# Attention and two gated MLPs on one core: the second MLP's projections in seven block products of 288 tokens

## The chip, the cores and the metric

The kernel runs on one core of one Trainium2 chip. The core's engines have queues of their own: TensorE (PE; its weight loads are PEld), VectorE (DVE), ScalarE (ACT), GpSimd (POOL) and SyncE (SP), which here only issues DMAs. The metric is the device time of one execution in microseconds; the median of several runs counts.

## The reference

Three parts follow one another, all in float32 with float64 weights:

```
attn:  q, k, v (4 batches, 8 heads, 576 positions, 64); heads 0-3 see the last 32 positions,
       heads 4-7 every 4th of the last 128
x   =  attn as 2304 tokens x 512
MLP 1: xn = x / sqrt(mean(x*x) + 1e-6) * rms_g
       g = xn @ w_gate;  v = xn @ w_val          (512 -> 1536)
       x = (g * sigmoid(g) * v) @ w_out          (1536 -> 512)
MLP 2: g = x @ w_gate;  v = x @ w_val
       out = (sigmoid(g) * v) @ w_out
```

Both MLPs have weights of their own. All matmuls of the MLPs need float32's precision.

## The kernel before

**Products.** A float32 operand is kept as two parts, a rounded one ("hi") and the rest ("lo"), and a product is three matmuls: hi·hi, hi·lo, lo·hi, in the format fp32r. The weights come as float64 words; `weight` (L302) turns them into float32 on the chip: ACT squares (L332), VectorE has four operations (L338, L341, L344, L347), then ACT rounds (L354, "whi") and GpSimd subtracts (L358, "wlo"), on tiles of 128 × 512.

**Tiles.** Tokens go in six chunks of 384, numbered 0 to 5. Each MLP runs in two passes; a pass holds six tiles of 128 hidden values and takes all six chunks with them. So there are four passes of 36 steps. In a step (`mlp_step`, L792 by way of `proj`) PE makes g and then v with 12 matmuls of 384 columns each; ACT takes tanh of g (L811), VectorE multiplies (L814, L819, L823), ACT or VectorE rounds the result (L826, L828, "hh") and GpSimd subtracts (L830, "hl"). After it PE makes the y of the step before (L855). In the first MLP y has the weights as the stationary operand and 384 tokens as columns, twelve matmuls in four banks. In the second MLP the hidden tile is stationary and 512 outputs are the columns, nine matmuls in three banks, so that the result lies in rows and goes straight to DRAM. Sums of a first pass go to DRAM and come back in the second (`part_load` L873, `y_evac` L884 to L914).

**Attention.** The 48 groups (four batches, four pairs of heads, thirds of a batch's positions) run in the prelude and in the first pass, ahead of the chunk that needs them. One group is a chain: scores on PE (L555), masks on VectorE (L566), exp on ACT (L572), sums and reciprocal (L579, L580), the product with it on GpSimd (L585), transposes on PE (L600), a copy (L604), values on PE (L612), a copy (L631). After the last group of a chunk comes `x_norm`: squares on ACT (L656), three additions on GpSimd (L664), sums over partitions by six matmuls of one column (L672), the reciprocal root on VectorE and GpSimd (L688 to L710), its spreading (L713) and turning on PE (L729), then xn, xh, xl (L740, L746, L751).

**Order.** `Line.emit` is a list scheduler. Each operation has a planned cost and a due time; at every step the operation that can start first is emitted, and of those that start alike the one due first. The order of g, v and y on PE is fixed by a key ("PE order"); attention, `x_norm` and the weights are put between by their due times from the table PARAMS (lo1 to hi5 are the due times of the groups for chunks 1 to 5). Each engine works off its queue in the emitted order.

## Time and profile before

| | |
|---|---|
| median of 3 runs | 1074.43 us (1071.85 to 1074.86) |
| profiled execution | 1074.17 us |
| its span | 1072.4 us |
| mean granted clock of PE | 0.971 |
| busy: PE, DVE, POOL, ACT | 1031.4, 499.3, 403.2, 353.9 us |
| prelude, up to the first step | 0 to 65.41 us |
| first pass | 65.41 to 379.10 us |
| second pass | 379.10 to 612.52 us |
| third pass | 612.52 to 840.62 us |
| fourth pass and the end | 840.62 to 1072.40 us |

A pass without a stall has 36 steps; in the first pass attention is added. The span is what the profile's records cover; the execution's own time holds 1.8 us more. In a row of the timeline a matmul's duration overlaps that of its neighbours; its cost is the distance of starts. The granted clock (PEclk) is 1.00 at 2.4 GHz and 0.50 at 1.2 GHz. In names such as `g<-xh,whi` the output stands ahead of the arrow and the operands behind it.

### The profile page before, as it was taken

The numbers are of one execution on the slowest core, as the hardware profiler recorded it, in microseconds if no ns is written. First come the engines' busy times: TensorE is split into PE (matmuls) and PEld (weight loads), VectorE is DVE, ScalarE is ACT, GpSimd is POOL, SyncE is SP. The second block draws the span as 40 slices with busy tenths as digits, with TensorE's granted clock in tenths as the row PEclk, the third lists the DMA queues.
The fourth block names the chain that finished last, engine by engine and source line by source line (L and its number), as shares of the span: only waits on it lengthen the run. The fifth ranks groups of instructions, "written<-read, shape, count | busy, mean of one in ns | idle before, by whom it ended". The sixth has DMA issues, their size and how long they took to land.

```text
span 1072.4 us, 17094 instructions
## 1 busy us (share of the span) xinstructions
PE 1031.4 (96%) x6455; PEld 967.7 (90%) x6455; DVE 499.3 (47%) x1080; ACT 353.9 (33%) x930; POOL 403.2 (38%) x536
## 2 busy tenths in 40 slices
PE   7889699999999899999999899999999999999998
PEld 6668589898999899999999889999999999999997
DVE  4699875554388988882226894101101111110111
ACT  4757544545233333332124332112214211111111
POOL 4556855344443743332135751111116411111111
PEclk8759999999999999999999899999999999999999
DMA  7858557441245355574225353102201211321210
GB/s 162 194 154 168 123 159 150 92 106 40 96 152 188 113 187 190 183 273 149 79 89 181 126 195 138 64 26 89 89 25 64 89 59 60 118 94 43 99 59 30
DMA packets 143538, 125.90 MB, mean 117 GB/s; under 512 B 94304, under 2 KB 128096, under 8 KB 143456
## 3 DMA queue, kind: packets, MB, share of 16 engines
q1 hardware_dynamic: 143456, 124.81, 38.2%
q8 instruction: 51, 0.84, 0.3%
q14 instruction: 31, 0.25, 0.1%
HBM read 91.75 MB, written 33.03 MB: 116 GB/s over the span
## 4 chain that ended last, share of the span: by engine, by line
PE 83%; DVE 9%; DMA 2%; issue 2%; POOL 2%; SPq 1%; ACT 1%; DVEq 0%; POOLq 0%; ACTq 0%
PE g L792 26%; PE v L792 25%; PE y L855 25%; PE att L555 2%; DVE wz L341 2%; DVE wz L344 2%; PE att L612 2%; DVE wz L338 1%; PE att L600 1%; DVE wz L347 1%; SPq L388 1%; SPq L463 1%; PE y L612 0%; DVE big L897 0%; DVE t L814 0%
## 5 line engine op out<-in xcount | busy, mean ns | idle before, releaser
L830 POOL TENSOR_TENSOR hl<-t,hh 128x384 fp32r<-128x384 f32 x141 | 152.1, 1079 | 530.2 <-ACT hh L826 491.8
L792 PE MATMUL g<-xh,whi 128*128 128x384 f32 x576 | 198.3, 344 | 7.4 <-DVE t L814 7.4
L823 DVE SCALAR_TENSOR_TENSOR t<-t,v 128x384 f32<-128x384 f32 x72 | 39.8, 553 | 354.7 <-PE v L792 348.7
L792 PE MATMUL g<-xh,wlo 128*128 128x384 f32 x576 | 196.5, 341 | 3.6 <-POOL wlo L358 3.6
L792 PE MATMUL v<-xh,whi 128*128 128x384 f32 x576 | 195.7, 340 | 2.1 <-DVE t L823 1.7
L792 PE MATMUL g<-xl,whi 128*128 128x384 f32 x576 | 195.6, 340 | 0.0
L792 PE MATMUL v<-xh,wlo 128*128 128x384 f32 x576 | 193.2, 335 | 0.9 <-POOL wlo L358 0.9
L792 PE MATMUL v<-xl,whi 128*128 128x384 f32 x576 | 193.1, 335 | 0.0
L811 ACT ACTIVATE t<-g 128x384 f32<-128x384 f32 x144 | 70.6, 490 | 313.7 <-PE g L792 298.4
L826 ACT CAST hh<-t 128x384 fp32r<-128x384 f32 x119 | 61.1, 513 | 239.3 <-DVE t L823 147.1
L792 PEld LDWEIGHTS g<-xh,whi 128*128 128x128 f32 x576 | 110.1, 191 | 12.8 <-DVE t L814 8.0
L358 POOL TENSOR_TENSOR wlo<-wz,whi 128x512 fp32r<-128x512 f32 x72 | 103.9, 1458 | 28.1 <-ACT whi L354 21.0
L792 PEld LDWEIGHTS g<-xh,wlo 128*128 128x128 f32 x576 | 110.2, 191 | 3.9 <-POOL wlo L358 3.9
L792 PEld LDWEIGHTS g<-xl,whi 128*128 128x128 f32 x576 | 110.3, 191 | 3.1
L792 PEld LDWEIGHTS v<-xh,whi 128*128 128x128 f32 x576 | 108.9, 189 | 4.2 <-DVE t L823 2.5
L792 PEld LDWEIGHTS v<-xh,wlo 128*128 128x128 f32 x576 | 108.6, 188 | 1.2 <-POOL wlo L358 1.2
L792 PEld LDWEIGHTS v<-xl,whi 128*128 128x128 f32 x576 | 108.8, 189 | 0.0
L855 PE MATMUL y<-hh,whi 128*128 128x384 f32 x288 | 101.0, 351 | 1.2 <-DVE ys L884 1.2
L855 PE MATMUL y<-hh,wlo 128*128 128x384 f32 x288 | 96.4, 335 | 0.0
L855 PE MATMUL y<-hl,whi 128*128 128x384 f32 x288 | 96.4, 335 | 0.0
L855 PE MATMUL y<-whi,hl 128*128 128x512 f32 x216 | 85.6, 396 | 0.0
L855 PE MATMUL y<-wlo,hh 128*128 128x512 f32 x216 | 85.3, 395 | 0.0
(125 smaller groups left out, 1501.9 us busy)
## 6 DMA issues: line engine op xcount, KB each, us to landing
wst<-in_moe_w_gate_dram SPq DMA_DIRECT2D x24, 512.0 KB
wst<-in_moe_w_val_dram SPq DMA_DIRECT2D x24, 512.0 KB
wst<-in_moe_w_out_dram SPq DMA_DIRECT2D x24, 512.0 KB
xh<-xh SPq DMA_DIRECT2D x12, 768.0 KB
xl<-xl SPq DMA_DIRECT2D x12, 768.0 KB
xh<-yh SPq DMA_DIRECT2D x12, 768.0 KB
xl<-yl SPq DMA_DIRECT2D x12, 768.0 KB
yp<-ys SPq DMA_DIRECT2D x24, 192.0 KB
```

What stands on the lines that cost most here:

```text
L338: add("DVE", 0.34, lambda: nc.vector.tensor_scalar(out=z.t.bitcast(F32), in0=z.t.bitcast(F32), scalar1=LEAST * LEAST, scalar2=MANTISSA, op ...
L341: add("DVE", 0.6, lambda: nc.vector.scalar_tensor_tensor(out=z.t, in0=top(), scalar=3, in1=z.t, op0=ALU.logical_shift_left, op1=ALU.bitwis ...
L344: add("DVE", 0.6, lambda: nc.vector.scalar_tensor_tensor(out=z.t, in0=top(), scalar=-0x40000000, in1=z.t, op0=ALU.bitwise_and, op1=ALU.bit ...
L358: add("PL", 1.23, lambda: nc.gpsimd.tensor_tensor(out=lo.t, in0=z.t.bitcast(F32), in1=hi.t.bitcast(F32), op=ALU.subtract), reads=[zk, ("hi ...
L555: nc.tensor.matmul(out=sc.t[r, u, :], lhsT=qt.t[r, p0:p0 + QB], rhs=kt.t[r, p0:p0 + WIN], start=True, stop=True)
L612: nc.tensor.matmul(out=o.t[64 * e:64 * e + 64, QB * u:QB * u + QB], lhsT=vt.t[:, G * g + u, e0 + e, :], rhs=pts.t[:, u, 64 * e:64 * e + 64 ...
L792: nc.tensor.matmul(out=bank.t, lhsT=l.t[:, s], rhs=r.t[:, kk], start=kk == 0 and n == 0, stop=kk == KD - 1 and n == 2)
L811: add("ACT", 0.37, lambda: nc.scalar.activation(out=t.t, in_=gb.t, func=ACTF.Tanh, scale=0.5), reads=[("bank", p, c, f, 0)], writes=[key], ...
L823: add("DVE", 0.47, lambda: nc.vector.scalar_tensor_tensor(out=t.t, in0=t.t, scalar=1.0, in1=vb.t, op0=ALU.add, op1=ALU.mult), reads=[("ban ...
L826: add("ACT", 0.41, lambda: nc.scalar.copy(out=hh.t, in_=t.t), reads=[key], writes=[("hh", p, c, f)], tiles=[t, hh], due=s + 0.6, other=() ...
L830: add("PL", 0.98, lambda: nc.gpsimd.tensor_tensor(out=hl.t, in0=t.t, in1=hh.t.bitcast(F32), op=ALU.subtract), reads=[key, ("hh", p, c, f)] ...
L855: nc.tensor.matmul(out=yb.t, lhsT=l, rhs=r, start=first and j == 0, stop=last and j == 2)
```

## The change

The first MLP keeps its matmuls, its two passes and its chunks of 384 tokens (T1, NF1). The second MLP is new:

- **Three passes** (TWO) of four hidden tiles each (NF), over the four batches, whose 576 tokens are two halves of 288 (T). Every other pass takes the batches in the opposite order, so that a pass begins with the operands that the one before ended with.
- **Seven products for eight.** `unit` takes two hidden tiles and two halves. With two blocks of the 512 input values, each of g and v is a 2 × 2 by 2 × 2 block product. Strassen's scheme (in Winograd's form) makes it of seven block products with sums of weight blocks (S1 to S4, `weight_blocks`) and of token blocks (T1 to T4, `x_blocks`). A block product is six matmuls of 288 columns. The seven use the banks X, Z, X, Y, X, Y, X: X is the bank g or v, Z and Y are two banks of "att". Products that belong to the same result add up in the bank; `snap` copies a bank (ACT, or VectorE), `plus` adds one to a copy (VectorE), `finish` takes tanh or multiplies and splits.
- **y** (`y_group`) has the weights as the stationary operand in this MLP too, three matmuls of 288 columns. The y of one batch is put between the products of the next; the first two units have none. The result lies turned: VectorE transposes blocks of 32 × 32 (`out_blocks`), and four DMAs for each tile write runs of 32 numbers; the last half is turned by PE (`out_rows`).
- **Weights aside.** `weight_ahead` converts a weight and stores the float32 tile to DRAM, `weight_load` reads it back when it is needed. It is used for the second half of the first MLP's weights (18, converted in the first pass) and for all 36 of the second MLP (converted in the second pass). Splits into hi and lo happen behind the reading (`split`), on half tiles of 256.
- **The plan.** Due times are now in microseconds (STEP is 6.24 for a step), costs are closer to measured ones, and the DMA is modelled as one bus. The due times of the attention groups are the old ones in the new unit.

The core of the diff:

```diff
-    17.458, "lo5": 29.921, "hi5": 18.146, "lead": -2.417, "xdue": 1.161, "wdue": -1.154,
...
+    "hi4": 108.9, "lo5": 186.7, "hi5": 113.2, "lead": -15.1, "xdue": 7.2,
...
+    ONE, TWO = 2, 3
+    NF1 = DF // P // ONE
+    NF = DF // P // TWO
...
+    def weight_ahead(p, f, i, load_due, due, release=0.0):
+        z = words(p, f, i, load_due, due, release)
+        key = (layer_of(p), f, i)
+        z_scr[key] = dr.tile([P, CW], F32, name=f"z{layer_of(p)}_{f}_{i}")
+        dma(lambda: nc.sync.dma_start(out=z_scr[key], in_=z.t.bitcast(F32)), 262e3,
+            reads=[("z", key)], writes=[("zs", key)], tiles=[z], due=due + 3)
+    def weight_load(p, f, i, due, early=False):
+        key = (layer_of(p), f, i)
+        z = new("sb", "wst", [P, CW], F32, NST) if early else one_of(Z_HOMES, [P, CW], F32)
+        dma(lambda: nc.sync.dma_start(out=z.t, in_=z_scr[key]), 262e3,
+            reads=[("zs", key)], writes=[("z", key), "zl order"], tiles=[z], due=due,
+            release=EARLY * early)
+        return z
+    EARLY = 285.0
+    def weight_late(p, f, i, due, early=False):
+        z = weight_load(p, f, i, due - 6, early)
+        if i == 2:
+            weight_out(p, f, z, lambda: z.t, due)
+        else:
+            weight_halves(p, f, i, z, lambda: z.t, due)
+    ORDER = ("11", "12", "S2", "S1", "S3", "S4", "22")
...
+    def weight_blocks(p, f, i, due):
+
+        layer = layer_of(p)
+        z = [weight_load(p, f + e, i, due - 6) for e in range(2)]
+        zk = [("z", (layer, f + e, i)) for e in range(2)]
+        blk = lambda e, k: lambda: z[e].t[:, k * KW:(k + 1) * KW]
...
+        for name in ORDER:
+            if name == "S2":
+                combine("S1", blk(1, 0), blk(1, 1), ALU.add, [zk[1]], [z[1]])
+                combine("S2", of("S1"), blk(0, 0), ALU.subtract,
+                        [("S", p, f, i, "S1"), zk[0]], [s_of["S1"], z[0]])
+            elif name == "S3":
+                combine("S3", blk(0, 0), blk(1, 0), ALU.subtract, zk, z)
+            elif name == "S4":
+                combine("S4", blk(0, 1), of("S2"), ALU.subtract,
+                        [("S", p, f, i, "S2"), zk[0]], [s_of["S2"], z[0]])
...
+    RIGHT = ("11", "21", "T2", "T1", "T3", "22", "T4")
...
+        for name in RIGHT:
+            if name == "11":
+                combine(lambda: t3.t, blk(1, 1), blk(0, 1), [key(1, 1), key(0, 1)], [tk],
+                        [xq[1], t3])
+                combine(blk(0, 1), blk(0, 1), blk(0, 0), [key(0, 0)], [key(0, 1)], xq)
+            elif name == "T2":
+                combine(blk(0, 0), blk(1, 1), blk(0, 1), [key(1, 1), key(0, 1)], [key(0, 0)], xq)
+            elif name == "T4":
+                combine(blk(1, 0), blk(1, 0), blk(0, 0), [key(0, 0)], [key(1, 0)], [xq[0]])
...
+    def y_group(p, c, f, m, due):
...
+        def products():
+            s = slice(m * P, m * P + P)
+            for j, (l, r) in enumerate(((0, 0), (0, 1), (1, 0))):
+                nc.tensor.matmul(out=yb.t, lhsT=w.t[:, l, s], rhs=h.t[:, r],
+                                 start=n == 0 and j == 0, stop=n == nf - 1 and j == 2)
...
+    def out_blocks(c, m, due):
+        src = parts[LAST, c]
+        t = new("sb", "ys", [P, T])
+        blocks = lambda x: x.rearrange("p (n i) -> p n i", i=32)
+        add("DVE", 0.5, lambda: nc.vector.transpose(
+            out=blocks(t.t), in_=blocks(src.t[:, m])), reads=[("sum", LAST, c, m)],
+            writes=[("ob", c, m)], tiles=[src, t], due=due + 1)
+        rows = out[c * T:(c + 1) * T, m * P:(m + 1) * P].rearrange(
+            "(n i) (a f) -> a i n f", i=32, f=32)
+        for a in range(4):
+            dma(lambda a=a: nc.sync.dma_start(
+                out=rows[a], in_=blocks(t.t[32 * a:32 * a + 32])), 37e3,
+                reads=[("ob", c, m)], writes=[("out", c, m, a)], tiles=[t], due=due + 2)
...
+            def product(i, bank, key, first):
+                l, r = wt[p, f, which, ORDER[i]], xop[p, b, RIGHT[i]]
+                def run():
+                    for j in range(2):
+                        cols = slice(j * P, j * P + P)
+                        for m, (a, d) in enumerate(((0, 0), (0, 1), (1, 0))):
+                            nc.tensor.matmul(out=bank.t, lhsT=l.t[:, a, cols], rhs=r.t[:, d, j],
+                                             start=first and j == 0 and m == 0,
...
+            steps = (("X", lambda: snap("11", X, "X")),
+                     ("Z", lambda: (plus("11", Z, "Z"), finish("11"))),
+                     ("X", lambda: snap("12", X, "X")),
+                     ("Y", lambda: snap("22", Y, "Y")),
+                     ("X", lambda: (plus("22", X, "X"), finish("22"))),
+                     ("Y", lambda: (plus("12", Y, "Y"), finish("12"))),
+                     ("X", lambda: finish("21")))
+            banks = [key for key, _ in steps]
+            for i, (key, then) in enumerate(steps):
+                product(i, {"X": X, "Y": Y, "Z": Z}[key], key, key not in banks[:i])
+                at += 0.78
+                then()
+                n += 1
+                while done < total * n // 14:
+                    at += extra[done](at, which)
+                    done += 1
...
+        for n in range(3 * NF1):
+            f, i = divmod(n, 3)
+            t = (8 + 24 * n / (3 * NF1)) * STEP
+            weight_ahead(1, NF1 + f, i, t - 8, t, 57 + 1.2 * t)
+            weight_late(1, NF1 + f, i, (NC1 * NF1 + f + (1.66 if i == 2 else i * 0.33) - 2) * STEP,
+                        n < 6)
+        todo = [(p, NF * (p - ONE) + 2 * u + e, i) for p in range(ONE, ONE + TWO)
+                for u in range(NF // 2) for i in range(3) for e in range(2)]
+        for n, (p, f, i) in enumerate(todo):
+            t = (NC1 * NF1 + 4 + 29 * n / len(todo)) * STEP
...
+        extra, carry = [[] for _ in range(NF // 2)], []
+        for p in range(ONE, ONE + TWO):
+            f0 = NF * (p - ONE)
+            for n, b in enumerate(range(B) if (p - ONE) % 2 == 0 else reversed(range(B))):
+                if n or p == ONE:
+                    x_blocks(p, b, at - 26)
+                else:
+                    for name in RIGHT:
+                        xop[p, b, name] = xop[p - 1, b, name]
+                        xkey[p, b, name] = xkey[p - 1, b, name]
+                for u in range(NF // 2):
+                    if not n:
+                        for i in range(2):
+                            weight_blocks(p, f0 + 2 * u, i, at - 24 + 8 * i)
+                        for e in range(2):
+                            weight_late(p, f0 + 2 * u + e, 2, at - 6)
+                    at = unit(p, b, u, at, extra[u])
+                extra, carry = late(p, b, carry)
+        for n, fn in enumerate(sum(extra, []) + carry):
+            at += fn(at, n % 2)
+
```

The order changes at two places that matter. The first is PE in the first pass, between chunk 4 and chunk 5. Before, the last attention group's scores (L555) stand there, between the matmuls of y (L855):

```order
L855 MATMUL y_3084<-hh,wlo 128x384
L555 MATMUL att<-kT,qT 64x96 x6
L855 MATMUL y_3095<-hh,whi 128x384
L855 MATMUL y_3095<-hl,whi 128x384
L855 MATMUL y_3095<-hh,wlo 128x384
L612 MATMUL att<-pts,v 64x64 x6
L855 MATMUL y_3123<-hh,whi 128x384
```

The spread reciprocal roots of that chunk (`rb`) are turned much later, also between matmuls of y:

```order
L792 MATMUL v<-xh,wlo 128x384
L855 MATMUL y_3817<-hh,whi 128x384
L855 MATMUL y_3817<-hl,whi 128x384
L855 MATMUL y_3817<-hh,wlo 128x384
L729 MATMUL att<-ident,rb 128x128 x3
L855 MATMUL y_3824<-hh,whi 128x384
L855 MATMUL y_3824<-hl,whi 128x384
L855 MATMUL y_3824<-hh,wlo 128x384
```

After, PE's queue at the same place reads as follows; L700 are scores, L742 the transposes of the probabilities, L754 the values, L814 the sums over partitions, L870 the turn of the roots, L973 the first g and v of chunk 5, L1010 y:

```order
L1010 MATMUL y_4261<-h,wo 128x384 x3
L1010 MATMUL y_4269<-h,wo 128x384 x3
L1010 MATMUL y_4274<-h,wo 128x384 x3
L1010 MATMUL y_4279<-h,wo 128x384 x3
L700 MATMUL att<-kT,qT 64x96 x6
L742 MATMUL att<-ident,pr 96x128 x3
L754 MATMUL att<-pts,v 64x64 x6
L814 MATMUL att<-ones,pt 128x1 x3
L870 MATMUL att<-ident,rb 128x128 x3
L973 MATMUL g<-xo,w 128x384 x12
L973 MATMUL v<-xo,w 128x384 x12
L1010 MATMUL y_4261<-h,wo 128x384 x3
```

The five operations of attention and normalization stand in five rows that follow one another, and the first g of the chunk stands right behind them.

The second place is PE in the second MLP. Before, a step ends with v (the last three of its 12 rows are shown) and has the y of the step before, with the hidden tile `hh`, `hl` as one operand:

```order
L792 MATMUL v<-xh,whi 128x384
L792 MATMUL v<-xl,whi 128x384
L792 MATMUL v<-xh,wlo 128x384
L855 MATMUL y_8328<-whi,hh 128x512
L855 MATMUL y_8328<-wlo,hh 128x512
L855 MATMUL y_8328<-whi,hl 128x512
L855 MATMUL y_8334<-whi,hh 128x512
L855 MATMUL y_8334<-wlo,hh 128x512
```

After, the first unit starts right behind the first MLP's last y, and its products (L1147) follow one another, each in another bank than the one before:

```order
L1010 MATMUL y_6913<-h,wo 128x384 x3
L1010 MATMUL y_6922<-h,wo 128x384 x3
L1147 MATMUL g<-xo,w 128x288 x6
L1147 MATMUL att<-xo,w 128x288 x6
L1147 MATMUL g<-xo,w_5414 128x288 x6
L1147 MATMUL att<-xo,w_5419 128x288 x6
L1147 MATMUL g<-wst,w_5434 128x288 x6
L1147 MATMUL att<-wst,w_5480 128x288 x6
L1147 MATMUL g<-wst,w 128x288 x6
L1147 MATMUL v<-xo,w 128x288 x6
```

From the third unit on a group of y (L1010) stands behind each product:

```order
L1147 MATMUL g<-xo_7333,w 128x288 x6
L1010 MATMUL y_7573<-h,wo 128x288 x3
L1147 MATMUL att<-xo_7337,w 128x288 x6
L1010 MATMUL y_7590<-h,wo 128x288 x3
L1147 MATMUL g<-xo_7455,w_5414 128x288 x6
L1010 MATMUL y_7603<-h,wo 128x288 x3
```

Six matmuls of 288 columns take the place of twelve of 384, and three of 288 stand between them where nine of 512 stood behind two projections.

## Rows read from the trace of the kernel before

**Rows 1.** The page: the chain that ended last, by engine.

```profile
PE 83%; DVE 9%; DMA 2%; issue 2%; POOL 2%; SPq 1%; ACT 1%; DVEq 0%; POOLq 0%; ACTq 0%
```

**Rows 2.** Windows by chunk: us, busy (count) of PE, PEld, DVE, ACT, POOL; PEclk.

```profile
65.41:141.11 75.70, 65.16 (x516) 54.61 (x514) 71.72 (x186) 45.31 (x147) 59.98 (x85) 0.87 0.62 146
...
298.83:336.27 37.44, 37.44 (x218) 37.44 (x217) 32.87 (x50) 13.31 (x26) 13.38 (x12) 1.00 0.46 152
336.27:379.10 42.83, 39.48 (x218) 38.84 (x218) 38.59 (x46) 16.12 (x31) 27.93 (x19) 0.96 0.47 155
...
567.76:612.52 44.76, 40.44 (x217) 40.12 (x217) 35.31 (x42) 19.38 (x37) 31.50 (x24) 0.92 0.43 149
612.52:652.62 40.10, 38.23 (x203) 35.51 (x203) 36.05 (x46) 15.04 (x29) 18.79 (x15) 1.00 0.54 182
652.62:840.62 188.00, 188.00 (x992) 176.22 (x991) 22.80 (x39) 43.10 (x86) 47.88 (x45) 1.00 0.18 68
```

**Rows 3.** Timeline of PE in layer 2: start, us, line, operation.

```profile
799.55 0.33 PE L792 MATMUL v<-xl,whi 128*128 128x384 f32 x1
...
800.93 0.39 PE L855 MATMUL y<-whi,hh 128*128 128x512 f32 x1
...
802.09 0.40 PE L855 MATMUL y<-whi,hl 128*128 128x512 f32 x1
```

**Rows 4.** Timeline of PE at matmuls of one column.

```profile
217.69 0.72 PE L672 MATMUL att<-ones,big 128*128 128x1 f32 x6
218.28 0.42 PE L792 MATMUL g<-xh,whi 128*128 128x384 f32 x1
```

**Rows 5.** Windows of an idle stretch and of what follows it.

```profile
592.00:597.00 5.00, 0.88 (x6) 0.56 (x4) 4.93 (x5) 0.00 (x0) 2.68 (x2) 0.93 0.31 105
597.00:603.00 6.00, 5.80 (x18) 5.80 (x19) 5.72 (x8) 3.13 (x6) 4.50 (x3) 0.50 0.23 87
```

**Rows 6.** Timeline of one attention group and one normalization: start, us, engine, line.

```profile
234.82 0.71 PE L555 MATMUL att<-kT,qT 64*64 64x96 f32 x12
...
237.64 0.99 POOL L585 TENSOR_SCALAR pr<-pr,rs 128x96 f32<-128x96 f32 x3 [0.91 <-DVE rs L580]
...
237.68 0.49 PE L600 MATMUL att<-ident,pr 128*96 128x128 f32 x3
...
238.32 0.47 ACT L604 COPY pts<-att 96x384 f32<-96x384 f32 x1
...
278.41 0.94 ACT L656 ACTIVATE big<-xT 128x384 f32<-128x384 f32 x2
...
279.43 3.20 POOL L664 TENSOR_TENSOR big<-big 128x384 f32<-128x384 f32 x3 [1.13 <-ACT big L656]
...
283.77 0.72 PE L672 MATMUL att<-ones,big 128*128 128x1 f32 x6
...
289.15 0.55 DVE L713 COPY rb<-rsy 128x384 f32<-128x384 f32 x1 [3.37 <-POOL rsy L710]
...
296.93 0.49 PE L729 MATMUL att<-ident,rb 128*128 128x128 f32 x3
...
298.83 0.33 PE L792 MATMUL g<-xh,whi 128*128 128x384 f32 x1
```

**Rows 7.** Groups by form: busy us, mean ns, idle before.

```profile
L341 DVE SCALAR_TENSOR_TENSOR wz<-wst,wz 128x512 int32<-128x512 int32 x72 | 67.3, 935 | 1.8
...
L338 DVE TENSOR_SCALAR wz<-wz 128x512 f32<-128x512 f32 x72 | 51.1, 712 | 18.6 <-ACT wz L332 14.0 <-POOL wz L335 4.2
...
L604 ACT COPY pts<-att 96x384 f32<-96x384 f32 x38 | 17.9, 473 | 20.4 <-PE att L600 20.0
```

**Rows 8.** Timeline: the last matmul into a bank, and its reader.

```profile
804.95 0.33 PE L792 MATMUL g<-xh,wlo 128*128 128x384 f32 x1
...
805.38 0.49 ACT L811 ACTIVATE t<-g 128x384 f32<-128x384 f32 x1 [3.08 <-PE g L792]
```

**Rows 9.** Timeline of SP's queue: one issue of 128 short runs.

```profile
240.79 0.59 SPq L473 DMA_DIRECT2D v<-in_v_dram  x1
```

More of the change, by code (lines that the diff above doesn't have):

```diff
@@ L167, in emit @@
             o.end = start + cost + o.lat
+            if o.bus:
+                self.bus = max(self.bus, start + cost) + o.bus
+                o.end = self.bus + o.lat
             for t in o.tiles:
@@ new lines, in y_group @@
+    def y_group(p, c, f, m, due):
+        layer = layer_of(p)
+        nf, width, cost = (NF, T, 0.39) if layer else (NF1, T1, 0.52)
+        n = f % nf
+        if (p, c) not in ybank:
+            ybank[p, c] = [new("ps", f"y{i}", [P, width], F32, 1) for i in range(KD)]
+        yb, w, h = ybank[p, c][m], wo[layer, f], htile[p, c, f]
+        def products():
[3 more added lines that the diff above has]
+                                 start=n == 0 and j == 0, stop=n == nf - 1 and j == 2)
+        add("PE", cost, products, reads=[("wo", layer, f), ("hs", p, c, f)],
+            writes=[("y", p, c, m), "PE order"], tiles=[yb, w, h], due=due)
+        if n == nf - 1:
+            (y_evac if layer else y_first)(p, c, m, due + 0.4)
@@ new lines, in part_load @@
+    def part_load(p, c, due):
+        if p == 0:
+            return
+        if p == 1:
+            t = parts[p, c] = new("sb", "pt", [P, KD, T1], F32, 2)
+            dma(lambda: nc.sync.dma_start(out=t.t, in_=y_part[c]), 786e3,
+                reads=[("part", 0, c, m) for m in range(KD)],
+                writes=[("sum", p, c, m) for m in range(KD)] + ["pt order"], tiles=[t], due=due)
+            return
+        t = parts[p, c] = new("sb", "pt", [P, KD, T], F32, 2)
+        if p > ONE:
+            dma(lambda: nc.sync.dma_start(out=t.t, in_=o_part[c]), 590e3,
+                reads=[("part", p - 1, c)], writes=[("sum", p, c, m) for m in range(KD)] +
+                ["pt order"], tiles=[t], due=due)
@@ new lines, in out_rows, with turn @@
+    def out_rows(c, t, which, due):
+        p = LAST
+        src = parts[p, c]
+        bank = new("ps", "vg"[which], [TQ, KD, P], F32, 1)
+        row = one_of(Z_HOMES, [TQ, DM], F32)
+        def turn():
+            for m in range(KD):
+                nc.tensor.transpose(bank.t[:, m], src.t[:, m, t * TQ:(t + 1) * TQ], ident)
+        add("PE", 0.45, turn, reads=[("sum", p, c, m) for m in range(KD)] + ["ident"],
+            writes=[("ob", c, t), "PE order"], tiles=[src, bank], due=due)
+        add("ACT", act(DM), lambda: nc.scalar.copy(
+            out=row.t, in_=bank.t.rearrange("p m o -> p (m o)")), reads=[("ob", c, t)],
+            writes=[("row", c, t)], tiles=[bank, row], due=due + 0.5,
+            other=("ys", "DVE", dve2(DM), lambda: nc.vector.tensor_copy(
+                out=row.t, in_=bank.t.rearrange("p m o -> p (m o)"))))
+        r0 = c * T + t * TQ
+        dma(lambda: nc.sync.dma_start(out=out[r0:r0 + TQ, :], in_=row.t), 197e3,
+            reads=[("row", c, t)], writes=[("out", c, t)], tiles=[row], due=due + 1)
@@ new lines, in whole @@
+        steps = ONE * NC1 * NF1
+        for n in range(3 * NF1):
+            f, i = divmod(n, 3)
+            t = (8 + 24 * n / (3 * NF1)) * STEP
[4 more added lines that the diff above has]
+                for u in range(NF // 2) for i in range(3) for e in range(2)]
```

685 lines of the change are left out of this document (392 added, 293 removed), and 2 rows, old and new, of the table PARAMS.

## The prediction, made before the changed kernel had run

> **What bounds the kernel now.** I read the chain that ended last first: 83% of it is TensorE's own matmuls and 9% is VectorE [rows 1]. So the time is the matmuls' columns plus the places where PE is kept waiting. The windows by chunk say where those places are [rows 2]. The row 652.62:840.62 (the last five chunks of the third pass) has PE busy 188.00 of 188.00 us at full granted clock: nothing but columns counts there. The row 298.83:336.27 is a layer-1 chunk without a stall, 37.44 us. Against these two, 336.27:379.10 (the last chunk of the first pass) is 5.4 us too long, 567.76:612.52 (the last of the second) 7.3 us, and 612.52:652.62 (the first of the third) 40.10 − 188.00/5 = 2.5 us. In all three VectorE is busy for 35 to 39 us: it converts the next pass's weight words there. The first row, 65.41:141.11, is 75.70 us long with VectorE busy 71.72: the first chunk is bound by VectorE, not by PE.
>
> The timeline gives the price of a column [rows 3]: eight matmuls of 384 columns from 799.55 to 800.93, 0.1725 us each, and five of 512 from 800.93 to 802.09, 0.232 each, so 0.449 and 0.453 ns per column with no fixed part to be seen. A matmul of one column cannot hide its weight load, and six of these take 0.59 us, 0.098 each [rows 4].
>
> **The second MLP's matmuls.** Before, a step has 24 matmuls of 384 columns and nine of 512, and there are 72 steps: 995,328 columns. After, 24 units have 14 products of six matmuls (2016), and 1152 more make y, all of 288 columns: 912,384 columns. That is 11/12: seven products for eight on the two thirds that are projections. Thirty steps in 188.00 us [rows 2] are 6.267 a step, 451.2 for 72; 11/12 of it is 413.6, **−37.6 us**, at 0.1306 us a matmul. The trace has no matmul of 288 columns with a full weight load. Its bounds: the load alone, 0.098 [rows 4], lies under 0.1306 and so cannot lengthen it; at the worst a matmul stays at the 0.1725 of 384 columns, 546 us, or +95. I take 0.1306, since the rows at 384 and 512 fall on one line through zero.
>
> A rule of the Trainium skill speaks against that. "TensorE: Matmul & The Clock Gate", section "Back-to-back issue gap", gives about 81 ns a matmul at 128 columns and 131 at 512 in a stream with weight loads, so a large part that does not shrink with the columns. By a straight line between these (an estimate from that page) layer 2 would take about 284 us before and 323 after: the 22% more matmuls would cost 40 us. The rows disagree, with 232 ns at 512.
>
> **Weights aside.** Layer 2's 36 weights, and 18 of layer 1, are now converted earlier (18 during the first pass, 36 during the second), stored to DRAM and read back. Four VectorE operations of 0.71 to 0.94 us [rows 7], about 3.5 us a weight, are as many as before; what changes is where they stand. In the second pass they are now spread, six per 37.4 us chunk (21 us of VectorE), so the stalls at the two boundaries, 7.3 + 2.5, should go; I leave 3 us for the start of the new stage, in which PE waits for the first turned banks and combinations: **−7**. The last chunk of the first pass loses its 5.4 us of waiting for conversions but still takes on splits: **−4**. In the first chunk VectorE keeps nearly all of its work (one conversion fewer, 3.5 us, others in place): −1.5. In chunks 1 to 3 fewer conversions save some, and chunk 1's normalization costs 3: its sums and its turn of the roots now have 1.9 us of matmuls between them, where 5.9 are needed [rows 6] and 5.5 stood before: −1. Together **−2.5**, between −8 and +6.
>
> **The last attention group.** This is a loss which the order of PE shows. Before, the last scores, the last sums and the last turn of the reciprocal roots stand in three places with tens of matmuls between. After, the last group's scores, its turn, its values, the sums and the turn of the roots follow one another on PE, with chunk 5's first g right behind and nothing between. Every link is then bare [rows 6]: scores at 234.82 to the end of the probabilities at 238.63, 3.8 us; transposes at 237.68 to the copy's end at 238.79, 1.1; values and their copy, about as long, 1.0; two squares 0.94; three GpSimd additions 3.20; the sums at 283.77 to the end of the spread roots at 289.70, 5.9; the turn at 296.93 to the first g at 298.83, 1.9. With a tenth of a microsecond for each of six hand-overs that is 18.4 us, of which PE works about 2. So some 16.5 us stand idle, and then the clock: after the idle stretch 592 to 597 the granted clock was 0.50 (1.2 GHz) for the next 6.0 us [rows 5], which gives away 3.0 us; I take 2. **+18.5.** Bounds: 14, if the additions start beneath the squares and the clock costs nothing, and 22 with the whole 3.0 and slower additions; a gain is excluded, since before waits for nothing there. What VectorE and GpSimd do of the weights in that time is counted in the chunk terms.
>
> **Turning banks over.** In a product's sequence the g or v bank is used four times, and between two uses there is one other product (6 × 0.1306 = 0.78 us) plus, from the third unit on, y work of the same length: 1.57. To turn a bank over, its reader starts 0.43 us after the start of the last matmul [rows 8], 0.30 after its end, and a copy of 384 elements takes 0.473 [rows 7], so 0.77 and a semaphore. In the first two units that is no slack at all in 16 places; a cast or a tanh ahead of the copy adds its 0.49 [rows 8]. I take 0.2 each, 3 us. In the other 176 places 0.8 us are to spare, one operation ahead in the queue is hidden and two are not; I take 4 us. **+7**, between 0 and +45 (0.25 each on 176).
>
> VectorE's turned output stands off PE. Its 112 transfers of 128-byte runs do not: SP needs 0.59 us for an issue with 128 runs [rows 9], these have 288, and 52 issues stand in the last 31 us, about all that SP can do. Behind the last chunk only three row transfers remain. **+1**, between 0 and +3.
>
> **Sum**, against the profiled execution's 1074.17 us (span 1072.4, and 1.8 around it): −37.6 − 7 − 4 − 2.5 + 18.5 + 7 + 1 = −24.6, that is 1049.6. The median of the runs shown, 1074.43, is 0.3 above that execution. **I forecast 1050 us.**
>
> **The rivals.** *The gap is given back.* VectorE and GpSimd work off in it what PE would wait for in other chunks, the boundaries lose all their 9.8 us, chunk 5 its 5.4, the other chunks 8, and no bank waits: 1074.2 − 37.6 − 9.8 − 5.4 − 8 + 14 + 1 = 1028. For it: PE waits in the first pass mostly for VectorE's conversions, which don't wait for PE; against it: conversions stand far ahead of the gap by then, and the first chunk, the worst, lies before it. Half-way cases reach 1042. Chance 0.17.
>
> *The banks wait more.* Mean waits of 0.12 us at 192 places are 23 instead of 7, so 1066 us, and with 0.15 it is 1072. For it: copies, tanh and casts share ACT, in order, and a bank is used again sooner than a projection's was; against it: in layer 2 ACT was busy 43 of 188 us [rows 2]. Chance 0.16, of which 0.05 within 0.3% of before.
>
> *The banks decide (the slower side).* Same place, but each of the 192 turnovers finds a reader queued behind an operation of about half a microsecond, 0.30 us on the mean: 58 instead of 7, 1101 us. The point from which the kernel is slower is 0.16 us a turnover (7 + 24.5 us over 192). Against it: 0.8 us of spare in 176 of them. Chance 0.07.
>
> *The narrow matmul does not shrink in full.* At 0.1384 us (6% more) the saving falls to 12.8 and with the chain's loss the change ends even; at 0.145, 459 us, it is 1095. The rows speak against it. Chance 0.03.
>
> **How the numbers follow.** The forecast itself, 1042 to 1061, has 0.57. 0.3% of 1074.4, 3.2 us, is about what a measurement can tell from no change. Faster than that: 0.57 + 0.17 + 0.11 = 0.85; within it 0.05; slower 0.07 + 0.03 = 0.10. The range that holds 8 in 10 leaves out the lower half of the first rival and the slower cases: 1034 to 1073.
>
> **What would show it.** Right: in layer 2 matmuls of 288 columns 0.130 apart; PE idle for 15 to 18 us in one stretch ahead of chunk 5 of the first pass, with a granted clock of 0.5 behind it; the second pass's last chunk near 37.4 us; layer 2 from its first product to the end near 424 us; waits of PE for ACT or VectorE copies in it below 10 us in sum. Wrong: a spacing over 0.138; PE waiting at most turnovers; PE at work under the last group's chain; the first pass more than 20 us above 314 (141.11 − 65.41 and the chunks behind it to 379.10).

## The result, and the profile after

The changed kernel takes 1080.6 us (median of 5, 1078.2 to 1082.3), 1.0059 times the kernel before (95% interval 1.0037 to 1.0080): slower by 0.6%, where 1050 us had been forecast. The profiled execution took 1078.5 us, with a span of 1076.7 us, 4.3 more than before.

The page's chain by engine, to be held against [rows 1]:

```profile
PE 71%; DVE 12%; DMA 4%; SPq 4%; issue 4%; POOL 3%; ACT 2%; DVEq 0%; POOLq 0%; ACTq 0%
```

PE's share of the chain fell from 83% to 71%: its matmuls have fewer columns in all, and it waits more. The windows say where; the columns are those of [rows 2], the first four rows are chunks 3, 4 and 5 of the first pass and the last chunk of the second, the next the first two units, the rest of the second MLP, and the end:

```profile
257.51:297.98 40.47, 40.47 (x254) 39.55 (x253) 24.78 (x52) 13.49 (x32) 16.38 (x26) 1.00 0.40 137
297.98:357.92 59.94, 46.24 (x307) 43.11 (x307) 21.01 (x56) 15.76 (x46) 16.79 (x33) 0.88 0.30 101
357.92:399.07 41.15, 40.49 (x216) 39.56 (x217) 12.62 (x22) 14.11 (x33) 18.49 (x21) 0.92 0.42 135
...
587.85:628.63 40.78, 40.11 (x229) 39.47 (x229) 37.77 (x52) 18.53 (x42) 30.90 (x29) 1.00 0.51 156
...
628.63:660.00 31.37, 24.37 (x168) 22.49 (x168) 28.54 (x44) 14.55 (x34) 21.11 (x16) 1.00 0.29 98
660.00:1070.46 410.46, 403.58 (x3015) 398.52 (x3013) 243.49 (x454) 168.77 (x401) 195.91 (x193) 1.00 0.31 93
1070.46:1076.70 6.24, 0.27 (x3) 0.01 (x1) 0.00 (x0) 0.64 (x2) 0.00 (x0) 0.79 0.53 130
```

Chunk 4 is 22.5 us longer than the 37.44 of an undisturbed one. Of these 18.6 are a bare chain at its end; the other 3.9 are the matmuls of two more attention groups, which the kernel before had in earlier chunks. The first MLP ends at 628.6 us, where it ended at 612.5 before. The second MLP takes 448.1 us to the end of the span against 459.9: of the 37.6 us expected for its matmuls, 11.8 came. In its first two units PE is idle for 7 of 31.4 us, while VectorE is busy for 28.5.

The bare chain ahead of chunk 5, on PE (start, duration, line, operation, and the idle time before it with what ended it):

```profile
339.34 0.71 PE L700 MATMUL att<-kT,qT 64*64 64x96 f32 x12
342.57 0.96 PE L742 MATMUL att<-ident,pr 128*96 128x128 f32 x3 [2.52 <-POOL pr L730]
344.09 0.91 PE L754 MATMUL att<-pts,v 96*64 96x64 f32 x12 [0.56 <-ACT pts L746]
349.60 1.44 PE L814 MATMUL att<-ones,pt 128*128 128x1 f32 x6 [4.60 <-POOL pt L806]
355.72 0.87 PE L870 MATMUL att<-ident,rb 128*128 128x128 f32 x3 [4.67 <-DVE rb L855]
357.92 0.69 PE L973 MATMUL g<-xo,w 128*128 128x384 f32 x1 [1.33 <-ACT xo L402]
```

From 339.34 to 357.92 it is 18.6 us, link by link as [rows 6] had it (3.8 to the probabilities, 3.1 for the additions, 6.0 from the sums to the spread roots). Behind it the granted clock was at half speed, 0.50 for 6.3 us; most of that lies in chunk 5:

```profile
339.80:356.20 16.40, 4.03 (x31) 3.01 (x26) 2.02 (x12) 2.91 (x10) 6.31 (x18) 0.62 0.24 85
356.20:362.50 6.30, 4.31 (x12) 2.99 (x11) 4.05 (x6) 2.05 (x4) 2.00 (x2) 0.50 0.47 152
```

A bank that is turned over late, in unit 3 (timelines of VectorE, of GpSimd and of PE):

```profile
689.86 1.42 DVE L404 CAST h<-t 128x288 fp32r<-128x288 f32 x1
691.20 0.44 DVE L1159 COPY t<-v 128x288 f32<-128x288 f32 x1
...
689.46 1.65 POOL L406 TENSOR_TENSOR xo<-T,xo 128x576 fp32r<-128x576 f32 x1
...
691.70 0.53 PE L1147 MATMUL v<-xo,w 128*128 128x288 f32 x2 [0.44 <-DVE t L1159]
```

The last matmul into bank v had ended by 689.7. VectorE could copy the bank only at 691.20, since it had begun a cast that takes 0.31 us by itself and took 1.42 beside GpSimd's subtraction; PE waited. The same picture stands in units 5, 11, 13, 19 and 21. Over the second MLP all gaps on PE sum to 20.5 us, 9.2 of them in the first two units. Nearly all of it, 19.4 us, lies at 23 places. Seventeen of these, 14.9 us with the slow restarts described below, end with a copy on VectorE (L1159), which does only 29 of the 144 copies. ScalarE (L1157) does the other 115, and three waits, 1.6 us, end with one of them. The view of PE's waits, which leaves out short ones and counts from a matmul's modelled end, shows the same order (us in total, times, longest):

```profile
PE v L1147 <- DVE t L1159: 4.4, 7, 1.6
PE g L1147 <- DVE t L1159: 3.1, 1, 3.1
PE att L1147 <- DVE t L1159: 1.9, 1, 1.9
...
PE g L1147 <- ACT t L1157: 0.4, 1, 0.4
```

The spacing of the new matmuls, in the run of y at the end:

```profile
1056.06 12.16 PE L1010 MATMUL y<-h,wo 128*128 128x288 f32 x90 [0.42 <-DVE pt L1077]
1068.06 0.63 PE L1113 MATMUL v<-ident,pt 128*96 128x128 f32 x3
```

These are 90 matmuls in 12.00 us, of which 0.11 is the slow restart described below: 0.132 us each.

### The profile page after: what moved, and what is told of

Read it like the earlier page. It is cut to its first block, busy times and chain, and to the rows that moved or that the text cites. A ratio compares the mean times of both kernels' runs of the same rounds, so it can differ in the third digit from the quotient of the medians.

```text
span 1076.7 us, 20044 instructions
## 1 busy us (share of the span) xinstructions
PE 1006.9 (94%) x7254; PEld 964.7 (90%) x7254; DVE 695.7 (65%) x1479; ACT 458.0 (43%) x1231; POOL 503.7 (47%) x659
## 4 chain that ended last, share of the span: by engine, by line
PE 71%; DVE 12%; DMA 4%; SPq 4%; issue 4%; POOL 3%; ACT 2%; DVEq 0%; POOLq 0%; ACTq 0%
PE y L1010 23%; PE g L973 12%; PE v L973 11%; PE att L1147 9%; PE g L1147 6%; PE v L1147 5%; SPq L612 1%; PE att L700 1%; DVE t L1180 1%; SPq L659 1%; PE att L754 1%; DVE h L404 1%; DVE wz L389 1%; DMA wst<-in_moe_w_val_dram 1%; DVE h L409 1%
## 5 line engine op out<-in xcount | busy, mean ns | idle before, releaser
L1010 PE MATMUL y<-h,wo 128*128 128x288 f32 (+1 forms) x2016 | 369.9, 313 | 2.0 <-POOL h L406 1.0
L1010 PEld LDWEIGHTS y<-h,wo 128*128 128x128 f32 x2016 | 318.5, 188 | 4.6 <-POOL h L406 1.6
L406 POOL TENSOR_TENSOR h<-t,h 128x288 fp32r<-128x288 f32 (+1 forms) x149 | 146.1, 983 | 303.8 <-ACT h L402 238.9
L973 PE MATMUL g<-xo,w 128*128 128x384 f32 x864 | 170.8, 345 | 5.5 <-DVE t L987 2.5
L973 PE MATMUL v<-xo,w 128*128 128x384 f32 x864 | 163.8, 337 | 0.0
L973 PEld LDWEIGHTS g<-xo,w 128*128 128x128 f32 x864 | 154.2, 193 | 10.0 <-DVE t L987 3.2
L973 PEld LDWEIGHTS v<-xo,w 128*128 128x128 f32 x864 | 150.4, 188 | 1.5
L1147 PE MATMUL att<-xo,w 128*128 128x288 f32 x576 | 92.7, 296 | 0.8
L1164 DVE TENSOR_TENSOR t<-t,att 128x288 f32<-128x288 f32 x96 | 43.4, 452 | 65.3 <-PE att L1147 61.6
L1147 PEld LDWEIGHTS att<-xo,w 128*128 128x128 f32 x576 | 81.4, 188 | 2.2 <-DVE t L1159 2.2
L392 DVE SCALAR_TENSOR_TENSOR wz<-wst,wz 128x512 int32<-128x512 int32 x72 | 67.7, 940 | 1.4
L1147 PE MATMUL v<-xo,w 128*128 128x288 f32 x396 | 64.1, 297 | 2.9 <-DVE t L1159 2.8
L717 ACT ACTIVATE pr<-pr,nmx 128x96 f32<-128x96 f32 x144 | 52.6, 367 | 28.5 <-DVE nmx L711 28.3
L1147 PE MATMUL g<-xo,w 128*128 128x288 f32 x396 | 63.2, 295 | 0.0
L395 DVE SCALAR_TENSOR_TENSOR wz<-wst,wz 128x512 int32<-128x512 int32 x72 | 60.5, 840 | 1.5
```

The costliest lines, as they stand in the source:

```text
L392: add("DVE", dve(CW), lambda: nc.vector.scalar_tensor_tensor(out=z.t, in0=top(), scalar=-0x40000000, in1=z.t, op0=ALU.bitwise_and, op1=ALU ...
L395: add("DVE", dve(CW), lambda: nc.vector.scalar_tensor_tensor(out=z.t, in0=low(), scalar=29, in1=z.t, op0=ALU.logical_shift_right, op1=ALU. ...
L406: add("PL", pool(n), lambda: nc.gpsimd.tensor_tensor(out=lo(), in0=src(), in1=hi().bitcast(F32), op=ALU.subtract), reads=reads, writes=[ke ...
L717: add("ACT", PARAMS["exp_cost"], lambda u=u: nc.scalar.activation(out=pr.t[:, u], in_=pr.t[:, u], func=ACTF.Exp, bias=nmx.t[:, u:u + 1], s ...
L973: nc.tensor.matmul(out=bank.t, lhsT=w[:, l, cols], rhs=x[:, r, j], start=kk == 0 and n == 0, stop=kk == KD - 1 and n == 2)
L1010: nc.tensor.matmul(out=yb.t, lhsT=w.t[:, l, s], rhs=h.t[:, r], start=n == 0 and j == 0, stop=n == nf - 1 and j == 2)
```

## The experiments

Ratios are to the kernel before, measured beside it on the same chip; PE's gaps in the second MLP are summed over the trace (distances of starts over 0.2 us, less 0.132; in e12_tail 1.6 us for twelve transposes that stand between are left out).

| run | median us | ratio, 95% interval | gaps in MLP 2, us (first two units) |
|---|---|---|---|
| changed kernel | 1080.6 | 1.0059 [1.0037, 1.0080] | 20.5 (9.2) |
| e1_chain | 1069.8 | 0.9962 [0.9940, 0.9984] | 24.3 (12.4) |
| e2_no_dve_split | 1074.8 | 1.0017 [0.9996, 1.0037] | 16.0 (7.6) |
| e4_eight | 1095.1 | 1.0203 [1.0173, 1.0233] | 0.0 |
| e5_recost | 1076.6 | 1.0018 [0.9999, 1.0037] | 23.6 (8.4) |
| e6_no_sums | 1072.7 | 0.9987 [0.9973, 1.0000] | 15.5 (6.8) |
| e7_replan | 1079.8 | 1.0057 [1.0036, 1.0077] | 29.6 (7.8) |
| e8_release | 1061.7 | 0.9887 [0.9872, 0.9901] | 19.6 (8.0) |
| e9_copies_first | 1050.8 | 0.9789 [0.9772, 0.9806] | 7.7 (4.3) |
| e10_first_nodve | 1051.2 | 0.9789 [0.9775, 0.9804] | 7.2 (2.4) |
| e11_first_alone | 1071.7 | 0.9983 [0.9967, 0.9999] | 13.7 (10.3) |
| e12_tail | 1048.9 | 0.9774 [0.9758, 0.9791] | 7.8 (4.3) |

My theory after the result: three faults of order (the bare chain, conversions that run into the last steps, and copies queued behind slower work) took back what the products saved. The rival: the seven products need more of VectorE than there is, in whatever order.

**The price of a matmul and of a cast, by themselves (p1_widths).**

```diff
+WIDTHS = (512, 384, 288, 256, 320, 352, 448, 192, 288, 384, 512)
+ROUNDS = 16
...
+        for n in WIDTHS:
+            for r in range(ROUNDS):
+                bank = banks[r % 4]
+                for j in range(6):
+                    c = slice((j % 4) * P, (j % 4) * P + P)
+                    nc.tensor.matmul(out=bank[:, 0:n], lhsT=w[:, c], rhs=x[:, 0:n],
+                                     start=j == 0, stop=j == 5)
```

> A probe instead of the kernel: back-to-back matmuls with a 128x128 weight tile each and 192 to 512 columns, 96 of a width; beside them VectorE casts and additions of 128x288, first alone, then with GpSimd subtracting beside them. It computes nothing of the reference. Theory (a column has one price): 288 columns 0.130 us, 384 0.173, 512 0.231, and 192 0.087 or the weight load, about 0.1, whichever is longer. Rival (each matmul has a part that does not shrink): 288 columns 0.132 or more, 192 columns well over 0.09. For VectorE: a cast from SBUF to SBUF takes 0.31 us alone and about 1.2 with GpSimd beside it; one that reads a PSUM bank stays at 0.45. Rival: GpSimd makes no difference and the long casts of the changed kernel had another cause.

This probe ran once. The spacing is taken from the starts of the first and the last of 96 matmuls at a granted clock of 1.00 (for 512 columns from the second set, since the first twelve matmuls of the probe came 0.427 us apart):

```
columns   192     256     288     320     352     384     448     512
us        0.111   0.120   0.132   0.147   0.160   0.173   0.203   0.227
```

The rival holds: 288 columns cost 0.132, not 0.130. From 448 to 352 columns the price is 0.45 ns a column; at 288 it is 0.458, at 256 0.469, at 192 0.58: the fewer columns, the less is saved. VectorE in the same run (groups by line: count, busy us, mean ns):

```profile
L51 DVE CAST d<-raw 128x288 fp32r<-128x288 f32 x16 | 12.3, 768 | 0.5
L53 DVE TENSOR_TENSOR e<-raw 128x288 f32<-128x288 f32 x12 | 11.9, 1060 | 0.0
...
L46 DVE CAST d<-raw 128x288 fp32r<-128x288 f32 x24 | 5.4, 308 | 4.2 <-DMA raw<-in_q_dram 4.2
L56 DVE TENSOR_TENSOR e<-raw,zb 128x288 f32<-128x288 f32 x12 | 4.5, 444 | 0.0
```

L46 is the cast alone (308 ns), L51 the same cast beside GpSimd (768), L53 an addition of two SBUF operands beside GpSimd (1060), L56 one with a PSUM operand, also beside GpSimd (444). The theory holds in direction; the 1.2 us of the cast is 0.77 on the mean here.

**The bare chain (e1_chain).**

```diff
-    "hi4": 108.9, "lo5": 186.7, "hi5": 113.2, "lead": -15.1, "xdue": 7.2,
+    "hi4": 108.9, "lo5": 113.2, "hi5": 168.0, "lead": -15.1, "xdue": 7.2,
```

> The changed kernel with the due times of chunk 5's attention groups rising (113 to 168 us) instead of falling (187 to 113), so that the last group no longer stands alone on PE ahead of chunk 5. Theory (the bare chain costs its whole length): the 18 us between 340 and 358 in which PE works for 2 us go, and the half-clock behind them: about 1061 us, 19 less than the changed kernel. Rival (VectorE and GpSimd used the gap for work that PE would wait for otherwise): at most 6 us less, about 1075.

The windows of chunks 3, 4 and 5 and of the second pass's last chunk in this run:

```profile
260.61:304.57 43.96, 43.96 (x308) 42.01 (x307) 29.45 (x71) 17.97 (x49) 18.75 (x32) 1.00 0.38 127
304.57:345.37 40.80, 40.58 (x254) 39.55 (x253) 20.40 (x42) 12.07 (x29) 15.84 (x28) 1.00 0.52 181
345.37:383.69 38.32, 37.73 (x217) 37.41 (x217) 9.90 (x18) 12.54 (x30) 16.80 (x20) 1.00 0.33 110
571.78:619.80 48.02, 42.30 (x230) 41.09 (x229) 45.42 (x60) 20.36 (x45) 35.85 (x32) 0.94 0.58 187
```

Chunks 3 to 5 together fell from 141.6 to 123.1 us: the chain, with the half clock behind it, cost 18.5. (Chunk 4 alone fell by 19.1, but two groups of attention went back from it into chunk 3.) But the second pass's last chunk grew from 40.8 to 48.0, with VectorE busy for 45.4 of it. In sum the gain is 10 us by the ratios, between theory and rival. The conversions of the second MLP may not start before a fixed planned time, so they did not move with the rest.

**Conversions earlier too (e8_release).**

```diff
-            weight_ahead(p, f, i, t - 8, t, t + 135)
+            weight_ahead(p, f, i, t - 8, t, t + 108)
```

> As the run with chunk 5's due times rising (e1_chain, 1069.8 us), with the earliest start of the second MLP's conversions 27 us earlier (t + 108 instead of t + 135). Theory (taking away the bare chain gained 19 us in its chunk and lost 10 at the end of the second pass, since the conversions are held back to a fixed time and ran into the last steps there): the last chunk of the second pass goes from 48.0 to about 39 us, 1061 us in all. Rival (VectorE has that work to do there anyway): 47 to 48 us, 1068 to 1071.

The result is 1061.7 us, and the last chunk of the second pass took 42.4 us instead of 48.0; the theory holds, if not quite to 39.

**Hidden values never split by VectorE (e2_no_dve_split).** The split of h in `finish` gets a kind of its own, for which the scheduler counts VectorE 50 us late.

```diff
+    ... "u_hi": 50.0, "u_lo": 50.0, ...
...
-                      ("hs", p, 2 * b + half, f + e), [tk], [], [t], at, "h")
+                      ("hs", p, 2 * b + half, f + e), [tk], [], [t], at, "u")
```

> The changed kernel with the hidden values of the second MLP split by ScalarE and GpSimd alone, never by VectorE (35 operations move). Theory (banks are turned over late because the copy on VectorE stands behind a cast that GpSimd beside it stretches to 1.4 us): the waits of 0.6 and 0.3 us in units 3, 5, 11, 13, 19 and 21 go, 7 us, and some of units 0 and 1: 1072 us. Rival (the engines beside PE are full, and the work is late wherever it goes): copies now wait behind casts on ScalarE, 1079 to 1085.

The gaps in units 3, 5, 11, 13, 19 and 21 went, 6.8 us, so their cause is the cast, or the subtraction behind it, ahead of the copy. VectorE still does 31 copies, and other gaps grew behind them: 3.8 us in unit 9 and 2.3 in unit 17. This is half of the theory's gain.

**Copies first (e9_copies_first; e11_first_alone).** In `snap` and `plus`, on top of e8_release:

```diff
-                    reads=[(key, uk)], writes=[ck[name]], tiles=[bank, t], due=at,
+                    reads=[(key, uk)], writes=[ck[name]], tiles=[bank, t], due=at - 1000,
...
-                    writes=[ck[name]], tiles=[bank, t], due=at)
+                    writes=[ck[name]], tiles=[bank, t], due=at - 1000)
```

> As e8_release, and the operations that empty a bank (the copies, and the additions of a bank to a copy) are given a due time far ahead, so that the scheduler lets an engine wait up to 0.34 us for them instead of starting something longer. Theory (banks are turned over late because of what the order puts ahead of the copy): waits in the second MLP fall from 21 to 24 us to below 14, 1053 us. Rival (the operations ahead of it are there already when the copy becomes ready): 18 us and more, no difference to e8_release.

The same second MLP, its first two units and the rest, and the end:

```profile
613.62:645.00 31.38, 29.25 (x204) 28.68 (x204) 25.89 (x41) 16.42 (x40) 22.84 (x20) 0.95 0.38 122
645.00:1042.26 397.26, 394.92 (x2978) 393.10 (x2977) 226.32 (x437) 171.00 (x412) 188.94 (x185) 1.00 0.31 94
1042.26:1049.30 7.04, 0.27 (x3) 0.02 (x1) 0.48 (x1) 0.65 (x2) 0.00 (x0) 0.77 0.53 124
```

The gaps are 7.7 us and the time 1050.8 us: better than the theory said. The operations of ScalarE, VectorE and GpSimd are 3369 as before, but some have changed engines: all 144 copies are now on ScalarE and none on VectorE, whose operations in the second MLP fall from 498 to 479. The place in unit 3 that was shown above, here on VectorE and on ScalarE:

```profile
670.37 1.42 DVE L404 CAST h<-t 128x288 fp32r<-128x288 f32 x1
...
669.91 0.40 ACT L1157 COPY t<-v 128x288 f32<-128x288 f32 x1 [0.51 <-PE v L1147]
```

The cast of 1.42 us is still there; the copy no longer stands behind it, and PE has no gap. So in these places it is the copy's engine that counts. How much the order among what stays on VectorE adds is not shown, since no run changes the one without the other. The edit alone:

> The changed kernel with nothing but the early due time for the operations that empty a bank (the edit of e9_copies_first alone); chunk 5's attention groups and the conversions' start as in the changed kernel. Theory (this edit and the other two are worth what they gave together, 11 us here and 19 there): waits in the second MLP from 20.5 to about 8 us, the bare chain of 18 us still there, 1069 us. Rival (the order of the second MLP only helps once the conversions are out of its first units): 1075 to 1080.

The result is 1071.7 us: 8 less by the ratios, again with all 144 copies on ScalarE. The gaps of the later units fell from 11.4 to 3.4 as in e9, but the first two units kept 10.3, most of it now behind VectorE's additions (L1164). So both statements hold in part: the edit helps in the later units, and the first two need the earlier conversions too.

**Both (e10_first_nodve).** As e9, with h split as in e2 and engines allowed to wait 0.6 us.

> As e9_copies_first, with engines let to wait 0.6 us and the hidden values of the second MLP split by ScalarE and GpSimd alone, as in e2_no_dve_split, where the waits of 0.6 and 0.3 us behind a slow VectorE cast went. Theory (the two causes add): waits below 10 us, 1050 us. Rival (ScalarE then has the copies and the casts and is late with both): 16 us and more, 1058 to 1064.

The result is 1051.2 us with gaps of 7.2: no gain over e9. With the copies on ScalarE it no longer matters here who casts.

**Eight products (e4_eight).**

```diff
-    ORDER = ("11", "12", "S2", "S1", "S3", "S4", "22")
+    ORDER = ("11", "12", "11", "12", "21", "22", "21", "22")
-    RIGHT = ("11", "21", "T2", "T1", "T3", "22", "T4")
+    RIGHT = ("11", "21", "12", "22", "11", "21", "12", "22")
...
+            bank_of = {"11": (X, "X"), "12": (Z, "Z"), "21": (Y, "Y"), "22": (X, "X")}
...
+            for i in range(8):
+                name = ("11", "12", "21", "22")[i // 2]
+                bank, key = bank_of[name]
+                product(i, bank, key, i % 2 == 0)
+                then = (lambda: finish(name)) if i % 2 else (lambda: None)
```

> The changed kernel with eight block products in the second MLP instead of seven: no sums of blocks, no copies of banks, each result in a bank of its own; all else as in the changed kernel. 288 matmuls of 288 columns more, 38 us by their spacing of 0.132 us. Theory (seven products save their columns, and lose 13 to 20 us again in bank waits): 38 less 13 to 20, so 1098 to 1106 us. Rival (the sums and copies cost what the eighth product would): 1076 to 1086.

```profile
629.98:665.00 35.02, 35.02 (x265) 35.02 (x265) 18.06 (x25) 15.12 (x36) 21.38 (x22) 1.00 0.59 191
665.00:1088.40 423.40, 422.84 (x3206) 422.14 (x3205) 102.34 (x218) 103.05 (x238) 114.62 (x123) 1.00 0.26 79
```

There is not one gap on PE. VectorE is busy for 120 us in this MLP, against 272 in the changed kernel. The second MLP is 16.2 us longer than there: 38.0 us of matmuls more, 20.5 us of gaps less, and 1.3 less at the end and in the spacing. By the ratios the whole is 15.5 us slower, a little under the theory's 18 to 25. So the seven products pay even as they stand, but only two fifths of what their columns save. Eight products were not run with the edits of e9.

**Without the sums of blocks (e6_no_sums).** The operations of `combine` are left out, and S1 to S4 and T1 to T4 are plain blocks, so that the output is another.

> The changed kernel without the sums of weight and token blocks (each of the seven products takes a plain block instead, so the second MLP's result is another). Products, splits, bank copies and the order of banks stay. Theory (VectorE's sums fill it in the first two units and behind each new batch, and copies stand behind them): waits in units 0 and 1 fall from 9.2 to 3 us, in the others from 11.4 to 5: about 1068 us. Rival (a copy takes too long for the time between two uses of a bank, whatever else VectorE does): waits stay above 16, 1077 or more.

The result is 1072.7 us with gaps of 15.5. The sums are a part of the trouble (5 us of gaps, and 2 in the first MLP), not the main one. The theory, with 8 us of gaps, falls. By its gaps the rival (16 us and more) comes nearly as written, but by its time the run lies between the two. What VectorE does besides the sums still delays its copies, 27 of them in this run.

**Other prices and another plan (e5_recost, e7_replan).** On top of e1_chain, VectorE's operations between SBUF operands on weights, splits and block sums are planned with these costs; e7_replan has other due times and preferences besides.

```diff
+    def dves(n):
+        return 0.155 + n / 660
+    def dve2s(n):
+        return 0.16 + n / 930
...
```

> As the run with chunk 5's due times rising (e1_chain, 1069.8 us), and the plan now prices VectorE's operations from SBUF to SBUF on weights, splits and block sums as the traces show them with GpSimd at work beside (0.155 + n/660 us instead of 0.155 + n/960, a cast 0.16 + n/930 instead of 0.155 + n/1920). Nothing is computed otherwise; only the order and the engine of these operations change. Theory (banks are turned over late since the plan puts more on VectorE than it can do in the time): the 24 us of waits in the second MLP fall below 14 and the 10.6 us too many at the end of the second pass halve: 1055 us. Rival (VectorE has too much to do there in any order): waits only move, 1066 to 1072.

> As the run with new prices (e5_recost), with other due times and preferences in the plan's table (attention groups, weights and block sums earlier or later, fewer splits on VectorE). Theory (what is lost is lost by the order, not by the work): 1045 to 1052 us. Rival (the plan's gains do not show on the chip): as e5_recost or worse.

Both theories failed: 1076.6 and 1079.8 us, with gaps of 23.6 and 29.6. With these prices chunk 0 took 86.3 and 85.7 us, where it took 79.6 in e1_chain, and VectorE still had 25 and 27 of the copies. Closer prices alone did not take the waits away; why the gaps grew in e7_replan is open.

**The end (e12_tail).**

```diff
-            if c < NCH - 1:
+            if c < NCH - 2:
                 out_blocks(c, m, due)
...
```

> As e9_copies_first (1050.8 us), with the last two halves of 288 tokens turned by PE and written as rows, instead of the last one: 16 fewer short transfers on SP and 12 more transposes on PE. Theory (at the end SP's queue is behind, since each of those transfers takes it 0.5 us): the 7.0 us from the last matmul's start to the end become 5, PE has 1.6 us more: 1050 us, no difference that can be measured. Rival (the end waits for the last sums alone): 1052 us.

The result is 1048.9 us; from the last matmul's start to the end it is 4.4 us instead of 7.0. The last rows had stood behind short transfers in SP's queue; in the changed kernel:

```profile
1061.12 9.42 SPq L1100 DMA_DIRECT2D out_dram<-ys  x16
1070.64 0.88 SPq L1123 DMA_DIRECT2D out_dram<-z  x2
1071.61 1.94 SPq L1100 DMA_DIRECT2D out_dram<-ys  x4
1073.64 0.40 SPq L1123 DMA_DIRECT2D out_dram<-z  x1
```

This is the fastest version, 0.9774 of the kernel before; its lead over e9 (0.9789) lies within both intervals.

## Why the prediction was wrong

The prediction summed to −24.6 us; the spans differ by +4.3. Step by step:

| step | predicted us | measured us |
|---|---|---|
| the second MLP's matmuls | −37.6 | −32.4 (3168 × 0.1322 against 451.2) |
| banks turned over | +7 | +20.5 |
| boundaries of the passes | −7 | −8.4 (4.0 at the second pass's end, and 4.4 us of gaps that the second MLP had before) |
| last chunk of the first pass | −4 | −4.5 (38.3 in e1_chain, without the half clock) |
| other chunks and the prelude | −2.5 | +6.1 (chunks 3 and 4 as in e1_chain) |
| the last attention group | +18.5 | +18.5 (chunks 3 to 5, against e1_chain) |
| the end | +1 | +4.5 (2.5 of transposes, 2.0 of SP's queue) |
| sum | −24.6 | +4.3 |

Of the 28.9 us between the two sums the banks are 13.5, the other chunks 8.6, the matmuls 5.2 and the end 3.5.

**The step that failed is "Turning banks over", +7 between 0 and +45.** It held that in 176 places "one operation ahead in the queue is hidden and two are not", with operations of half a microsecond. Those durations were ScalarE's, a copy and a tanh that read a PSUM bank [rows 7, rows 8]; VectorE's queue was not priced. In the kernel 29 of the 144 copies are on VectorE, and the trace and p1_widths show that there one operation is enough: a cast or sum on SBUF beside GpSimd takes 0.8 to 1.5 us, which is all the slack. PE's waits for these copies are 14.9 of the 20.5 us. With all copies on ScalarE (e9, e11) the gaps of the later units fall to 3.4 us.

The Trainium skill has the rule which I did not weigh: "SBUF — State Buffer", section "Who interferes with whom", says that a VectorE operation with two SBUF inputs, or a copy or cast in a two-port mode, shares a port pair with GpSimd, and that in a two-port mode whoever issues first keeps it for the whole instruction. The trace agrees: the cast of 1.42 us ended 0.17 us after GpSimd's instruction did, and the operations with a PSUM operand stayed at 0.44.

The mean wait was 0.11 us a turnover, near the 0.12 of the rival "the banks wait more". In its reason that rival was lucky: it argued from copies, tanh and casts that share ScalarE, and behind ScalarE's copies PE lost 1.6 us. It also spread the waits over all 192 turnovers, where nearly all the time was lost at 23 places.

**The other chunks were taken 8.6 us too low.** "In chunks 1 to 3 fewer conversions save some" had the wrong sign: VectorE's busy time there rose from 79.6 to 109.0 us. In chunks 0 to 2 PE is idle for 18.4 us, against 10.5 before, mostly ahead of matmuls of attention and normalization. No run takes these waits away, so their cause stays open. The split of the first pass between this row, the last chunk and the last group is an estimate, since it takes chunks 3 to 5 from e1_chain, where attention's order differs in other places too. The prediction's own sign of being wrong, a first pass more than 20 us above 314, came true with 335.2.

**The products were priced 1% too low.** "The rows at 384 and 512 fall on one line through zero" was true of these rows and not below them (0.132 at 288). The rival of the matmul that does not shrink in full was right in kind, at 0.132 instead of the 0.1384 where it would have decided. The Trainium skill's "TensorE: Matmul & The Clock Gate", section "LDWEIGHTS (loading the stationary operand)", has a formula by which a load of 128 columns takes 107 ns (an estimate from that page). The 0.111 at 192 columns lies near it and the 0.098 of [rows 4] below it; no run shows whether the load is what holds the price up. The second MLP has 33% more matmuls than before (3168 for 2376), not the 22% that the prediction names; its sum does not use that figure.

**The chain was right, in its links and in its price.** Chunks 3 to 5 of e1_chain are 18.5 us shorter, of which 2.8 is the half clock in chunk 5. The rival "the gap is given back" got a part: with the chain away, 7 us of this went again at the second pass's end. That was since a start time was fixed, as e8 shows, and not since VectorE had used the gap.

**The end was under-priced**: the twelve transposes were not counted, and the queue's backlog was taken at 1 us.

With 20.5 us for the banks the forecast would have been 1063, within its own range of 1034 to 1073; the rest of the miss is in the smaller steps of the list.

## What to carry to other kernels

In this kernel the scheme that trades matmuls for copies was limited by the slack of each bank, not by the busy share of the engines: write down for each bank the time from the last matmul to its next use, and put into it the longest operation that can stand ahead of the copy, at its contended length. Keep operations that free a bank out of a queue in which long ones can stand ahead of them. Here an early due time, by which every copy went to ScalarE, was worth 8 us alone and 11 on top of e8_release, and no operation was saved. When one wait is taken away, look for start times that were fixed against the old schedule.

## What the runs showed of the hardware

- A matmul in fp32r with a new weight tile each gets dearer by the column below 352 columns: 0.173 us at 384, 0.132 at 288, 0.120 at 256, 0.111 at 192.
- After PE has waited for a bank, the second matmul comes 0.238 us after the first instead of 0.132: each wait costs 0.11 us more than its length. In the second MLP of the changed kernel this follows each of the 23 waits named above, 2.4 us in all.
- A VectorE cast of 128 × 288 takes 0.308 us alone and 0.768 on the mean beside GpSimd (up to 1.43 in the changed kernel), an addition of two SBUF operands 1.06 beside GpSimd. With a PSUM operand it takes 0.444 beside GpSimd, and in the changed kernel at most 0.46.
